# A W added beside the second layer: when its two weights are multiplied, and who makes the denominators

## The chip, the cores and the metric

The kernel runs on one core of a Trainium2 chip. The metric is device time in microseconds (us) of one execution; three executions of the kernel before are at hand. Engines: TensorE (PE; PEld is its weight load), VectorE (DVE), ScalarE (ACT), GpSimd (POOL) and SyncE (SP, which issues DMAs). Each works through its own queue in order; semaphores join them.

## The reference

Two parts, the second fed by the first.

```python
batch, n_heads, seq, head_dim = (4, 4, 1088, 32)   # r = 8
def phi(x):                       # S1, S2: 8 x 32
    a = np.einsum('rd,bhsd->bhsr', S1, x)
    b = np.einsum('rd,bhsd->bhsr', S2, x)
    return np.einsum('bhsi,bhsj->bhsij', a, b).reshape(*x.shape[:-1], r * r)
q_p, k_p = (phi(q), phi(k))
kv = np.einsum('bhsf,bhsd->bhfd', k_p, v)
z = np.sum(k_p, axis=2)
num = np.einsum('bhsf,bhfd->bhsd', q_p, kv)
den = np.einsum('bhsf,bhf->bhs', q_p, z)[..., None] + 1e-06
attn = num / den
x = attn.transpose(0, 2, 1, 3).reshape(4352, 128)
h = x @ w_in                      # 128 x 2048
g = h - np.tanh(h)
out = g @ w_out                   # 2048 x 128
```

All tensors are float32. Since g @ w_out = x @ (w_in @ w_out) + tanh(-h) @ w_out, the kernel computes a small product W = w_in @ w_out once (as the sum of two bf16 halves, `whi` and `wlo`) and adds x W to the second layer of the tanh.

## The kernel before

The 4352 rows go through in 11 groups of 8 to 16 blocks of 32 rows (`GROUPS`, L304), so a group is 256, 448, 384, 448, 384, 512, 448, 384, 448, 384 and 256 columns wide. A batch is 34 blocks, so groups 0, 3, 5 and 8 are the first that need a new batch's keys.

For a batch (`keys`, `sums_of`): K comes by DMA into `kraw`, VectorE turns it in 32x32 blocks into `kT` (L537), PE projects it (L544), VectorE turns the result into `kab` (L555), VectorE and GpSimd make the 64 products per row into `wk` (L570), and PE sums them with V in 36 matmuls (L609). ACT copies the sums (`kvz`, L617), PE turns them (L620), ACT copies them again (`ndw`, L623). Beside this, a small sum of key products (L581, L593) is reduced (L596) into the weights `wq` of the query projection.

For a group (`project_q`, `q_ab`, `q_products`, `numerators`, `x_of`): VectorE turns Q (L631), PE projects it (L653), VectorE turns the projection into `qq` (L682), multiplies and adds to `dn` (L685, L688). One fp32 matmul with a fixed 0/1 matrix `qsum` adds pairs of 32-row blocks of `dn` (L697); VectorE takes the reciprocal (L700), scales (L704); GpSimd, and in groups called `half` VectorE for one of two halves, multiplies out `qp` (L716); VectorE turns it (L723); PE makes the numerators, which are x (L669); x is cast to bf16 into `xT` (L731), by ACT in the first two groups and by VectorE after that.

Then the layers (`layers`): 16 times a first-layer matmul into one of three PSUM banks (L792), a tanh on ACT into one of 40 slots (L795), and 12 slots later a second-layer matmul that accumulates in one PSUM bank, `acc` (L805). x W is two matmuls with `whi` and `wlo` into the same accumulator (L784), at its front, or at its end in the first group. VectorE turns the result out of `acc` into `osb` (L812), and SP stores it (L818). In the last group the layout is different (`last_rows`, L830).

W is made in the opening: the eight chunks of each half of `w_in` are turned by PE (`linear_turn`, L754), the first half into the bank of `acc`, copied by ACT (L759), multiplied with `w_out` by PE (L768), and split by VectorE into `whi` and `wlo` (L772, L773). The weights come as float32; ACT casts w_in in four pieces (L739), GpSimd w_out in two (L743).

The order on each engine is made when the program is built: every operation has an estimated cost and a due time (`prio`), and a list scheduler places it; `P.line([...])` forces an order by hand over named operations (`x0` is the first group's x, `t0_2` the third tanh of the first group, `ds0` its denominator matmul, `wk00` the first key product). `DUE_W` is the due time of the product W in units of 16 per group. Filler matmuls on a zero tile `wz` (L483, L489, L494) stand where PE would else be idle; the scheduler drops those for which there is no room.

Of the kernel before, what the change touches and what calls it, by code (L numbers as in the profile page):

```python
# [8 lines left out]
ALU = mybir.AluOpType  # L9
# [295 lines left out]
DUE_W = 23  # L305


def bass_polysketch_attn__then__act_tanh_shrink_kernel(nc, q, k, v, S1, S2, moe_w_in, moe_w_out, out):
# [40 lines left out]
    dn = [sb(f"dn{i}", [128, 32]) for i in range(2)]  # L349
    an = [sb(f"an{i}", [128, 32, 4]) for i in range(2)]  # L350
# [11 lines left out]
    osl = sb("osl", [128, 3, 128])  # L362
    osb = [sb(f"osb{i}", [128, G]) for i in range(2)]
# [328 lines left out]
    def q_products(g, T):  # L692
        u, n = g % 2, 2 * groups[g][1]
        m, a = n // 2, qq[u]
        half = g < 2 or g in first
        p_rd, p_an = ps[:, 0, 288:288 + n], ps[:, 1, 256:256 + 4 * m].rearrange("p (n x) -> p n x", x=4)
        P.op("tensor", 200, lambda e: e.matmul(  # L697
            ps[:, 0, 256:256 + n], qsum[:, :, :, :].rearrange("p u y j -> p (u y j)"), dn[u][:, 0:n], start=True, stop=True),
            r=[("qsum",), ("dn", u)], w=[bank[0]], prio=T - 0.5, tag=f"ds{g}")
        P.op("vector", 60 + 8.3 * n, lambda e: e.reciprocal(p_rd, ps[:, 0, 256:256 + n]),  # L700
             r=[bank[0]], w=[bank[0]], prio=T, tag=f"rd{g}")
# [25 lines left out]
    def x_of(g, T):  # L727
        _, nb, x0 = groups[g]
        nh = nb // 2
        early = g < 2  # L730
# [6 lines left out]
    def casts():  # L737
        for x in range(4):
            P.op("scalar", act(512), lambda e, x=x: e.copy(  # L739
                w_in[:, 512 * x:512 * x + 512], w_in_f[:, 512 * x:512 * x + 512]),  # L740
                r=[("w_in_f", x // 2)], w=[("w_in", x)], prio=(-50, -50, 2.5, 5.5)[x], tag=f"cin{x}")
# [5 lines left out]
    def linear_turn(half, T):  # L747
        bv, bk = (ps[:, 2, :], bank[2]) if half else (acc, ka)
# [14 lines left out]
    def linear_product(T):  # L763
        wp, kw = ps[:, 3, 0:128], bank[3]

        def product(e):
# [8 lines left out]
            r=[kw, ("whi",)], w=[("wlo",)], prio=T)  # L775

    def layers(g):
# [10 lines left out]
        for jb in range(NJB):  # L788
# [5 lines left out]
                r=[("w_in", jb // 4), ("xT", g)], w=[kb], prio=s, tag=f"h{g}_{jb}")  # L794
# [5 lines left out]
        if g:  # L800
            lin(True)
        for jb in range(NJB):
# [4 lines left out]
                start=(jb == 0 and not g), stop=(jb == NJB - 1 and bool(g))),  # L807
                r=[("w_out", jb // 8), ("t", ts)], w=[ka], prio=s + LAG)
        if not g:
            lin(False)  # L810
        u = g % 2
        P.op("vector", dve(n), lambda e: e.transpose(out=osb[u][:, 0:n], in_=acc[:, 0:n]),  # L812
             r=[ka], w=[("osb", u)], prio=slot0)
        ob = out.rearrange("(b j c) e -> b j c e", b=B, j=32)
        o = 0
        for b, c, nb in parts:
            for cb in range(4):
                P.op("sync", 4096 * nb / 250, lambda e, b=b, c=c, nb=nb, cb=cb, o=o: e.dma_start(  # L818
                    out=ob[b, :, c:c + nb, 32 * cb:32 * cb + 32],
                    in_=osb[u][32 * cb:32 * cb + 32, 32 * o:32 * (o + nb)].rearrange("p (c x) -> p c x", x=32)),  # L820
                    r=[("osb", u)], sem=f"out{u}", prio=slot0)
            o += nb
# [48 lines left out]
    for g in range(NG):  # L871
# [21 lines left out]
        if g == 1:  # L893
            layers(0)
        for x in range(1, B):
# [11 lines left out]
        if g:  # L907
# [49 lines left out]
```

## Time and profile before

| | us |
|---|---|
| three executions | 106.97, 108.19, 109.53; median 108.19 |
| the profiled execution | 107.36 |
| its span, first to last instruction | 105.6 |
| first tanh starts | 14.79 |
| last tanh ends | 101.81 |
| VectorE busy | 65.9 |

The granted clock of TensorE is 1.0 throughout. In a profile line of a timeline stand the start and the duration in us, engine, source line, operation, output <- input, shape, and a count where several were merged; in brackets the engine's idle time before it and what ended that. The busy time of PE is no measure of how full it is, as matmuls overlap in it; starts that follow each other show the rate.

### The profile page before, as it was taken

How to read it: one execution, taken by the hardware profiler on the slowest of the kernel's cores; microseconds unless marked ns; L12 is line 12 of the kernel's file. 1: busy time of each engine (PE TensorE's matmuls, PEld its weight loads, DVE VectorE, ACT ScalarE, POOL GpSimd, SP SyncE). 2: the span in 40 equal slices, each digit the busy share in tenths (PEclk: the TensorE clock that was granted, in tenths of full speed). 3: DMA queues.
4: the chain of work that ended last, by engine and by line, in shares of the span. 5: the costliest groups of instructions: out<-in, count | busy, mean ns of one | idle time of the engine just before them, and what ended most of it. 6: DMA issues, size and time to landing. Idle time of an engine off the chain costs nothing.

```text
span 105.6 us, 3129 instructions
## 1 busy us (share of the span) xinstructions
PE 101.1 (96%) x1285; PEld 54.0 (51%) x1288; DVE 65.9 (62%) x164; ACT 80.3 (76%) x193; POOL 33.3 (32%) x59
## 2 busy tenths in 40 slices
PE   6999999999999999999999999999999999999990
PEld 4535456583456454546546334454754634545580
DVE  3558996499944599783777478769186547143030
ACT  0004559999957977976989998797698998999950
POOL 5569427061811102870400700395030060120000
PEclk9999999999999999999999999999999999999999
DMA  2999999800199322016995022001400502203233
GB/s 68 313 284 281 361 274 252 228 16 0 34 284 241 139 42 45 6 30 107 302 262 100 0 33 48 0 3 25 67 14 4 89 0 43 35 0 58 35 48 76
DMA packets 23678, 11.21 MB, mean 106 GB/s; under 512 B 17648, under 2 KB 22384, under 8 KB 23664
## 3 DMA queue, kind: packets, MB, share of 16 engines
q1 hardware_dynamic: 20144, 7.44, 30.4%
q10 hardware_dynamic: 3520, 3.57, 11.1%
q8 instruction: 10, 0.16, 0.7%
q14 instruction: 4, 0.03, 0.1%
HBM read 8.78 MB, written 2.23 MB: 104 GB/s over the span
## 4 chain that ended last, share of the span: by engine, by line
PE 88%; ACT 9%; DVE 0%; issue 0%
PE ps L792 28%; PE ps L805 24%; ACT tt L795 8%; PE ps L483 6%; PE ps L669 5%; PE ps L609 4%; PE ps L653 4%; PE ps L784 3%; PE ps L544 3%; PE ps L830 2%; PE ps L697 2%; PE ps L494 1%; PE ps L581 1%; PE ps L768 1%; PE ps L754 1%; PE ps L593 1%
## 5 line engine op out<-in xcount | busy, mean ns | idle before, releaser
L795 ACT ACTIVATE tt<-ps 128x448 bf16<-128x448 f32 (+3 forms) x176 | 73.7, 527 | 8.0 <-PE ps L792 7.2
L792 PE MATMUL ps<-xT,w_in 128*128 128x448 bf16 (+3 forms) x174 | 55.9, 333 | 0.4
L805 PE MATMUL ps<-tt,w_out 128*128 128x448 bf16 (+3 forms) x159 | 49.4, 336 | 0.1
L792 PEld LDWEIGHTS ps<-xT,w_in 128*128 128x128 bf16 x176 | 16.8, 97 | 24.1 <-ACT tt L795 15.0
L716 POOL TENSOR_TENSOR qp<-an,qq 128x384 f32<-128x384 f32 (+3 forms) x17 | 14.5, 854 | 39.1 <-DVE an L704 38.3
L805 PEld LDWEIGHTS ps<-tt,w_out 128*128 128x128 bf16 x160 | 16.4, 102 | 8.2 <-issue 0.4
L570 POOL TENSOR_TENSOR wk<-kab 128x256 f32<-128x256 f32 (+1 forms) x18 | 12.6, 698 | 18.1 <-DVE kab L555 17.0
L723 DVE STREAM_TRANSPOSE qpT<-qp 128x448 f32<-128x448 f32 (+3 forms) x22 | 12.3, 577 | 5.2 <-POOL qp L716 5.0
L812 DVE STREAM_TRANSPOSE osb<-ps 128x448 f32<-128x448 f32 (+3 forms) x10 | 6.0, 598 | 7.8 <-PE ps L792 4.2
L700 DVE RECIPROCAL ps<-ps 128x28 f32<-128x28 f32 (+3 forms) x11 | 3.5, 315 | 10.4 <-PE ps L697 10.4
L682 DVE STREAM_TRANSPOSE qq<-ps 128x448 f32<-128x448 f32 (+3 forms) x11 | 6.3, 577 | 3.2 <-PE ps L653 3.1
L483 PE MATMUL ps<-wz 128*128 128x256 bf16 (+1 forms) x28 | 7.3, 398 | 1.1 <-DVE hmask L460 1.1
L617 ACT ACT_TABLE_LOAD x1 | 1.3, 1283 | 8.3 <-DVE gm L588 8.3
L631 DVE STREAM_TRANSPOSE qT<-qraw 128x256 f32<-128x256 f32 (+2 forms) x12 | 6.4, 531 | 1.2 <-DMA qraw<-in_q_dram 1.1
L731 DVE CAST xT<-ps 128x384 bf16<-128x384 f32 (+3 forms) x9 | 5.5, 608 | 1.3 <-PE ps L669 1.1
L669 PE MATMUL ps<-qpT,ndw 64*32 64x224 f32 (+3 forms) x176 | 6.2, 339 | 0.0
L537 DVE STREAM_TRANSPOSE kT<-kraw 128x576 f32<-128x576 f32 (+1 forms) x8 | 5.5, 722 | 1.0 <-DMA kraw<-in_k_dram 1.0
L653 PE MATMUL ps<-qT,wq 64*32 64x224 f32 (+3 forms) x176 | 6.1, 333 | 0.0
L570 DVE TENSOR_TENSOR wk<-kab,ps 128x512 f32<-128x512 f32 (+1 forms) x8 | 5.1, 638 | 0.0
L609 PE MATMUL ps<-wk,vx 128*32 128x64 f32 x288 | 5.1, 221 | 0.0
L609 PEld LDWEIGHTS ps<-wk,vx 128*32 128x32 f32 x288 | 4.2, 110 | 1.3 <-issue 1.3
L555 DVE STREAM_TRANSPOSE kab<-ps 128x576 f32<-128x576 f32 x4 | 3.1, 783 | 2.3 <-PE ps L544 2.3
(74 smaller groups left out, 82.7 us busy)
## 6 DMA issues: line engine op xcount, KB each, us to landing
kraw<-in_k_dram SPq DMA_DIRECT2D x3, 544.0 KB, 4.7
qraw<-in_q_dram SPq DMA_DIRECT2D x3, 544.0 KB, 6.1
vx<-in_v_dram SPq DMA_DIRECT2D x10, 144.0 KB, 4.0
w_in_f<-in_moe_w_in_dram ACTq DMA_DIRECT2D x2, 512.0 KB, 7.3
w_out_f<-in_moe_w_out_dram ACTq DMA_DIRECT2D x2, 512.0 KB, 8.4
out_dram<-osb SPq DMA_DIRECT2D x16, 56.0 KB, 1.9
out_dram<-osb SPq DMA_DIRECT2D x16, 48.0 KB, 1.8
vx<-in_v_dram SPq DMA_DIRECT2D x4, 112.0 KB, 5.1
```

The source lines that it names most:

```text
L483: P.op("tensor", 213 if x < 16 else 221, lambda e, n=1 if x < 16 else 2: e.matmul(ps[:, 3, 0:256 * n], wz[:, 0:128], wz[:, None, :].to_bro ...
L570: P.op(eng, (dve if eng == "vector" else pool)(64 * n), lambda e: e.tensor_tensor(out=wk[:, t0:t1, :, :].rearrange("p t h (i j) -> p (t h) ...
L609: ins = e.matmul(ps[32 * h:32 * h + 32, sbk, 0:64], vx[i][:, h, t, :], wk[:, t, h, :], start=(t == 0), stop=(t == 8), tile_position=(0, 32 ...
L631: P.op("vector", dve(hi - lo), lambda e, i=b % 2, lo=lo, hi=hi: e.transpose(out=qT[i][:, lo:hi], in_=qraw[i][:, lo:hi]), r=[("qraw", b % 2 ...
L653: ins = e.matmul(o, wq[64 * r:64 * r + 64, b, y, :, :].rearrange("p h x -> p (h x)"), src, start=True, stop=True, tile_position=(64 * r, 3 ...
L669: ins = e.matmul(ps[32 * h:32 * h + 32, 2 + u, 0:32 * nh], ndw[i][64 * u:64 * u + 64, 32 * h:32 * h + 32], src[64 * u:64 * u + 64, h // 2, ...
L682: P.op("vector", dve(16 * n), lambda e: e.transpose(out=a[:, 0:n, :].rearrange("p (r m) x -> p r (m x)", r=2), in_=ps[:, pb[0]:pb[1] + 1:p ...
L716: P.op("vector" if dv else "gpsimd", (dve if dv else pool)(32 * m), lambda e, lo=lo, dv=dv: e.tensor_tensor(out=qp[u][:, lo:lo + m, :].rea ...
L723: P.op("vector", dve(32 * m), lambda e, lo=lo: e.transpose(out=qpT[u][:, 32 * lo:32 * (lo + m)], in_=qp[u][:, lo:lo + m, :].rearrange("p n ...
L792: P.op("tensor", pe(n), lambda e, jb=jb, bk=bk: e.matmul(bk[:, 0:n], w_in[:, 128 * jb:128 * jb + 128], xT[:, t0:t0 + n], start=True, stop= ...
L795: P.op("scalar", act(n), lambda e, ts=ts, bk=bk: e.activation(out=tt[:, ts, 0:n], in_=bk[:, 0:n], func=AF.Tanh, scale=-1.0), r=[kb], w=[(" ...
L805: P.op("tensor", pe(n), lambda e, jb=jb, ts=ts: e.matmul(acc[:, 0:n], w_out[:, jb, :], tt[:, ts, 0:n], start=(jb == 0 and not g), stop=(jb ...
```

## The change

Five things are edited.

- W: both turns of `w_in` are now one due time, `DUE_W - 3` with `DUE_W` = 33 in place of 23, and use PSUM banks 2 and 3; the product uses bank 2. They come after the third group's x, and `acc` is no longer borrowed.
- The first group's x W no longer goes into its accumulator. The second-layer sum is turned into a new buffer `osx`; after W is there, x W is computed into bank 2, turned into `osb`, and GpSimd adds `osx`; then the first group is stored. The second group's x W moves to the end of its accumulation.
- Denominators: except in groups 0, 1, 4 and 7, VectorE copies `dn` with neighbouring 32-row blocks exchanged into PSUM (four copies) and adds `dn` into `sd`, of which it takes the reciprocal. Groups 6 and 9 are added to the `half` groups.
- The first x is cast in two halves, by ACT and VectorE; the second by VectorE; the fourth piece of w_in is cast by GpSimd.
- The orders forced by hand change: among others `wk02`, `u0`, `wk00` in place of `wk00`, `u0`, `wk02`.

```diff
-DUE_W = 23
+DUE_W = 33
+TURNED = (0, 1, 4, 7)
...
-        half = g < 2 or g in first
+        half = g < 2 or g in first or g in (6, 9, )
...
+        if g in TURNED:
+            P.op("tensor", 200, lambda e: e.matmul(
+                ps[:, 0, 256:256 + n], qsum[:, :, :, :].rearrange("p u y j -> p (u y j)"), dn[u][:, 0:n], start=True, stop=True),
+                r=[("qsum",), ("dn", u)], w=[bank[0]], prio=T - 0.5, tag=f"ds{g}")
+        else:
+            def swap(e):
+                for s in range(4):
+                    ins = e.tensor_copy(ps[32 * s:32 * s + 32, 0, 256:256 + n], dn[u][32 * (s ^ 1):32 * (s ^ 1) + 32, 0:n])
+                return ins
+
+            P.op("vector", 4 * 140, swap, r=[("dn", u)], w=[bank[0]], prio=T - 0.5, tag=f"ds{g}")
+            P.op("vector", dve(n), lambda e: e.tensor_tensor(
+                out=sd[u][:, 0:n], in0=dn[u][:, 0:n], in1=ps[:, 0, 256:256 + n], op=ALU.add),
+                r=[("dn", u), bank[0]], w=[("sd", u)], prio=T - 0.5, tag=f"dt{g}")
...
-        early = g < 2
+        if g == 0:
+            for half, eng in ((0, "scalar"), (1, "vector")):
+                P.op(eng, (act if eng == "scalar" else dve)(32 * nh), lambda e, half=half, eng=eng: (e.copy if eng == "scalar" else e.tensor_copy)(
+                    xT[:, x0 + 32 * nh * half:x0 + 32 * nh * (half + 1)], ps[:, 2 + half, 0:32 * nh]),
+                    r=[bank[2 + half]], w=[("xT", 0) if half else ("xT", -1)], prio=T, tag=("x0", "x0b")[half])
+            return
+        early = False
...
-            P.op("scalar", act(512), lambda e, x=x: e.copy(
+            P.op("scalar" if x < 3 else "gpsimd", act(512) if x < 3 else 650, lambda e, x=x: (e.copy if x < 3 else e.tensor_copy)(
...
-        bv, bk = (ps[:, 2, :], bank[2]) if half else (acc, ka)
+        bv, bk = ps[:, 2 + half, :], bank[2 + half]
...
-        wp, kw = ps[:, 3, 0:128], bank[3]
+        wp, kw = ps[:, 2, 0:128], bank[2]
...
+    def first_linear(T):
+        n = 32 * groups[0][1]
+        for x, nm in ((whi, "whi"), (wlo, "wlo")):
+            P.op("tensor", pe(n), lambda e, x=x, nm=nm: e.matmul(
+                ps[:, 2, 256:256 + n], x[:, :], xT[:, 0:n], start=(nm == "whi"), stop=(nm == "wlo")),
+                r=[(nm,), ("xT", 0), ("xT", -1)], w=[bank[2]], prio=T, tag="lin0" + nm)
+        P.op("vector", dve(n), lambda e: e.transpose(out=osb[0][:, 0:n], in_=ps[:, 2, 256:256 + n]),
+             r=[bank[2]], w=[("osb", 0)], prio=T, tag="olin0")
+        P.op("gpsimd", pool(n), lambda e: e.tensor_tensor(
+            out=osb[0][:, 0:n], in0=osb[0][:, 0:n], in1=osx[:, 0:n], op=ALU.add),
+            r=[("osb", 0), ("osx",)], w=[("osb", 0)], prio=T, tag="oadd0")
+        store(0)
...
-                start=(jb == 0 and not g), stop=(jb == NJB - 1 and bool(g))),
+                start=(jb == 0 and g < 2), stop=(jb == NJB - 1 and g != 1)),
...
+        ob, ok = (osb[u], ("osb", u)) if g else (osx, ("osx",))
+        P.op("vector", dve(n), lambda e: e.transpose(out=ob[:, 0:n], in_=acc[:, 0:n]),
+             r=[ka], w=[ok], prio=slot0)
...
-            linear_turn(0, 3)
             warm_more(40, 5001)
-            linear_turn(1, DUE_W - 3)
-            linear_product(DUE_W)
...
+        if g == 2:
+            linear_turn(0, DUE_W - 3)
+            linear_turn(1, DUE_W - 3)
+            linear_product(DUE_W)
+            first_linear(DUE_W + 4)
+            layers(1)
...
-    P.line(["kT00", "wkm", "kT01", "kab0", "kps0", "s2m", "gm0", "qT0", "wk00", "u0", "wk02", "qq0", "au0", "dn0", "qT1",
-            "rd0", "an0_1", "an0_0", "qp00", "qpT00", "qpT01", "qq1", "au1", "dn1", "qT2",
-            "rd1", "an1_1", "an1_0", "qp10", "qpT10", "qpT11", "qq2", "au2", "dn2", "rd2", "an2", "kT10", "kT11", "qpT21", "qpT20", "qT3"])
+    P.line(["kT00", "wkm", "kT01", "kab0", "kps0", "s2m", "gm0", "qT0", "wk02", "u0", "wk00", "qq0", "au0", "dn0", "qT1",
+            "rd0", "an0_1", "an0_0", "qp00", "qpT00", "qpT01", "qq1", "x0b", "au1", "dn1", "qT2",
+            "rd1", "an1_1", "an1_0", "qp10", "qpT10", "qpT11", "x1", "qq2", "au2", "dn2", "ds2", "dt2", "rd2", "an2", "kT10", "kT11", "qpT21", "qpT20", "qT3"])
...
-    P.line(["w0", "h0_2", "ds1", "wt0", "w1", "p2"])
+    P.line(["w0", "h0_2", "ds1", "w1", "p2"])
...
-    P.line(["t0_6", "cin3"])
-    P.line(["t0_5", "wc0"])
-    P.line(["wk03", "wk05", "wk07", "qp01", "cout0", "qp11", "cout1"])
+    P.line(["wk03", "wk05", "wk07", "qp01", "cout0", "cin3", "qp11", "cout1"])
```

More of the change, by code (lines that the diff above doesn't have):

```diff
@@ L775, in linear_product, with store @@
             r=[kw, ("whi",)], w=[("wlo",)], prio=T)
+    def first_linear(T):
[10 more added lines that the diff above has]
+        store(0)
+    def store(g):
+        ob = out.rearrange("(b j c) e -> b j c e", b=B, j=32)
+        o, u = 0, g % 2
+        for b, c, nb in groups[g][0]:
+            for cb in range(4):
+                P.op("sync", 4096 * nb / 250, lambda e, b=b, c=c, nb=nb, cb=cb, o=o: e.dma_start(
+                    out=ob[b, :, c:c + nb, 32 * cb:32 * cb + 32],
+                    in_=osb[u][32 * cb:32 * cb + 32, 32 * o:32 * (o + nb)].rearrange("p (c x) -> p c x", x=32)),
+                    r=[("osb", u)], sem=f"out{u}", prio=NJB * g)
+            o += nb
     def layers(g):
@@ L799, in layers @@
             return last_rows(g)
-        if g:
+        if g > 1:
             lin(True)
```

28 lines of the change are left out of this document (9 added, 19 removed).

## The prediction

> **What bounds the kernel now.** I read the page first: shares of busy time and the chain of waits.
>
> ```profile
> span 105.6 us, 3129 instructions
> ...
> PE 101.1 (96%) x1285; PEld 54.0 (51%) x1288; DVE 65.9 (62%) x164; ACT 80.3 (76%) x193; POOL 33.3 (32%) x59
> ...
> PE 88%; ACT 9%; DVE 0%; issue 0%
> PE ps L792 28%; PE ps L805 24%; ACT tt L795 8%; PE ps L483 6%; PE ps L669 5%; PE ps L609 4%; PE ps L653 4%; PE ps L784 3%; PE ps L544 3%; PE ps L830 2%; PE ps L697 2%; PE ps L494 1%; PE ps L581 1%; PE ps L768 1%; PE ps L754 1%; PE ps L593 1%
> ```
>
> The chain is nearly all TensorE, but a chain that goes back along the queue of PE also counts matmuls that had room. So the second view is the timeline of ACT alone from the first tanh on (start, duration, what, idle before).
>
> ```profile
> 14.79 0.94 ACT L795 ACTIVATE tt<-ps 128x256 bf16<-128x256 f32 x3 [0.38 <-PE ps L792]
> ...
> 16.91 1.06 ACT L759 COPY w_inT<-ps 128x1024 bf16<-128x1024 bf16 x1
> 17.80 0.46 ACT L795 ACTIVATE tt<-ps 128x256 bf16<-128x256 f32 x1
> 18.08 0.68 ACT L739 CAST w_in<-w_in_f 128x512 bf16<-128x512 f32 x1
> 18.59 0.46 ACT L795 ACTIVATE tt<-ps 128x256 bf16<-128x256 f32 x1
> 18.86 0.61 ACT L731 CAST xT<-ps 128x448 bf16<-128x448 f32 x1
> 19.27 2.42 ACT L795 ACTIVATE tt<-ps 128x256 bf16<-128x256 f32 x8
> 21.71 1.01 ACT L759 COPY w_inT<-ps 128x1024 bf16<-128x1024 bf16 x1
> 22.62 4.24 ACT L795 ACTIVATE tt<-ps 128x448 bf16<-128x448 f32 x9
> 27.08 2.73 ACT L795 ACTIVATE tt<-ps 128x448 bf16<-128x448 f32 x6 [0.22 <-PE ps L792]
> ...
> 30.73 0.54 ACT L795 ACTIVATE tt<-ps 128x448 bf16<-128x448 f32 x1 [0.93 <-PE ps L792]
> 32.10 0.27 ACT L617 COPY kvz<-ps 128x128 f32<-128x128 f32 x1 [0.82 <-PE ps L609]
> 32.52 0.49 ACT L795 ACTIVATE tt<-ps 128x384 bf16<-128x384 f32 x1 [0.16 <-PE ps L792]
> ...
> 33.06 4.36 ACT L795 ACTIVATE tt<-ps 128x384 bf16<-128x384 f32 x11
> 37.83 0.49 ACT L795 ACTIVATE tt<-ps 128x384 bf16<-128x384 f32 x1 [0.41 <-PE ps L792]
> ```
>
> Three stages show. From 14.8 to 27 us ACT never rests: the opening is bound by ACT, which does two casts and two copies of the transposed weight among its tanh. From 29.8 to 33 it rests 1.9 us in three holes: PE is behind, with the second batch's sums. Then eleven tanh of the third group run without a break, 4.36 / 11, about 0.39 us each. The rest of the kernel repeats this: a stretch of tanh without a break, then a rest at the turn of the group, as the 0.41 at 37.83.
>
> TensorE's queue at the places that matter, and VectorE's and GpSimd's:
>
> ```profile
> 17.24 0.93 PE L494 MATMUL ps<-wz 128*128 128x256 bf16 x7
> ...
> 18.10 0.61 PE L669 MATMUL ps<-qpT,ndw 64*32 64x224 f32 x16
> ...
> 21.07 0.61 PE L754 MATMUL ps<-identb,w_in 128*128 128x128 bf16 x8
> ...
> 22.84 1.06 PE L768 MATMUL ps<-w_out,w_inT 128*128 128x128 bf16 x16
> ...
> 29.61 0.61 PE L653 MATMUL ps<-qT,wq 64*32 64x224 f32 x16
> ...
> 30.82 1.21 PE L609 MATMUL ps<-wk,vx 128*32 128x64 f32 x72
> ...
> 37.45 0.34 PE L792 MATMUL ps<-xT,w_in 128*128 128x384 bf16 x1
> ```
>
> ```profile
> 1.07 0.41 DVE L462 MEMSET hmask<- 32x1 f32 x4
> ...
> 8.33 0.65 DVE L570 TENSOR_TENSOR wk<-kab,ps 128x512 f32<-128x512 f32 x1
> ...
> 8.90 0.18 DVE L596 TENSOR_REDUCE wq<-ps 128x16 f32<-128x32 f32 x1
> ...
> 9.00 0.40 DVE L570 TENSOR_TENSOR wk<-kab,ps 128x256 f32<-128x256 f32 x1
> ...
> 19.15 0.58 DVE L682 STREAM_TRANSPOSE qq<-ps 128x384 f32<-128x384 f32 x1 [1.42 <-PE ps L653]
> ...
> 20.06 0.28 DVE L688 TENSOR_REDUCE dn<-au 128x24 f32<-128x120 f32 x1
> ...
> 21.15 0.32 DVE L700 RECIPROCAL ps<-ps 128x24 f32<-128x24 f32 x1 [0.81 <-PE ps L697]
> ...
> 21.68 1.36 DVE L537 STREAM_TRANSPOSE kT<-kraw 128x576 f32<-128x576 f32 x2
> ...
> 24.68 0.25 DVE L772 CAST whi<-ps 128x128 bf16<-128x128 f32 x1
> ...
> 25.22 0.78 DVE L555 STREAM_TRANSPOSE kab<-ps 128x576 f32<-128x576 f32 x1
> ...
> 26.08 3.44 POOL L570 TENSOR_TENSOR wk<-kab 128x256 f32<-128x256 f32 x5 [2.47 <-DVE kab L555]
> ...
> 28.03 0.41 DVE L812 STREAM_TRANSPOSE osb<-ps 128x256 f32<-128x256 f32 x1
> ```
>
> Seven filler matmuls on a zero tile (L494) stand at 17.24: PE has time to give away where ACT binds. VectorE rests 1.42 us before 19.15 and is then busy without a break through the second batch's keys.
>
> **Opening, up to the first tanh.** The 256-wide key product now goes before the folded weight's reduction and the 512-wide one behind it: the reduction starts 0.65 - 0.40 = 0.25 us earlier, and the first group's projection waits for it. Two filler matmuls ahead of that projection go, so PE is free in time. The first x is split between ACT and VectorE, worth under 0.1 us; VectorE's half stands before the second group's sums of products and delays those by about what the earlier start gave. I take 0.25: first tanh at 14.54.
>
> **ACT's load up to the second group.** By distances between starts: the fourth cast of w_in (now GpSimd's) 18.59 - 18.08 = 0.51; the second x (now VectorE's) 19.27 - 18.86 = 0.41; the two copies of the transposed weight (moved back) 17.80 - 16.91 = 0.89 and 22.62 - 21.71 = 0.91. Together 2.72, so by ACT alone the second group's tanh would start at 22.62 - 0.25 - 2.72 = 19.65. PE has the work ready: the first group's second-layer matmuls now stand between its first-layer ones where fillers stood, since their accumulator no longer holds the transposed weight. The next bound is the second x: its numerators ran at 18.10 behind fillers and come no earlier now, because the thirteenth first-layer matmul stands ahead of them. They end at 18.71; a copy of 0.61 (ACT's row; VectorE's reads the same bank) ends near 19.4; the first layer and the way from matmul to tanh (37.45 to 37.83, 0.38) give a start at 20.2. That is 2.4 us earlier than before. GpSimd's cast stands behind the first half of w_out and well before the 448-wide product it must not delay; the addition of x W is one more 256-wide GpSimd operation (3.44 / 5 = 0.69), and only the first store waits for it.
>
> **What becomes of those 2.4 us.** The 15 tanh of the second group at about 0.45 end near 27.2, and ACT then makes the two copies (1.8 us) and three more tanh, to 30.3. There it must wait. In the emitted order PE now has projection, sums, weight product and the turn of kvz in one row, and only then three first-layer matmuls. The sums need GpSimd's five products, which begin when VectorE has turned the keys. VectorE's queue before that: out go the two halves of W (25.22 - 24.68 = 0.54); in come the second x (its 0.61, of which some 0.35 falls into the rest before 19.15; 0.25 is left), the first group's transpose into the extra buffer (0.41), and the third group's denominators. The last replaces a wait of 0.81 by four copies of 32 rows and one addition. No such copy is in the trace; bounds are the four 32-row memsets (0.41 for four) and four times the small PSUM reduction (4 x 0.18 = 0.72), plus 0.2 for the addition: 0.6 to 0.9, I take 0.75, nearer the reduction, which also touches PSUM. Net -0.54 + 0.25 + 0.41 - 0.06 = about 0: the keys are turned at 25.2 as before, and GpSimd ends at 29.5 as before. So the front of the queue gained 2.4 us and its tail nothing. The sums, 30.82 before, follow the projection directly: between 29.7 and 30.5 (the turn of w_in, 2 x 0.61 at most, now also stands ahead of them). They take 1.2, the product 0.9 to 1.06, the turn 0.3, and the third tanh of the third group starts between 32.6 and 33.3, against 33.06 + 0.39 = 33.45 before. Gain 0.15 to 0.8; I take 0.5. From there ACT binds both kernels up to the group's turn, where the fourth group's numerators now also wait behind VectorE's transpose of x W (0.41): I keep 0.4.
>
> [...]
>
> **Behind that.** The emitted order from the fourth group's projection on is the old one without the removed matmuls, and with two turns changed. The denominators' matmuls hold 2% of the chain, 2.1 us for 11: seven are worth at most 1.3, and nothing where unbroken tanh follow them. I take 0.3. VectorE has room, since it waited for most of them:
>
> ```profile
> DVE ps L700 <- PE ps L697: 10.4, 7, 2.4
> ...
> 63.44 0.60 ACT L795 ACTIVATE tt<-ps 128x512 bf16<-128x512 f32 x1 [0.19 <-PE ps L653]
> ```
>
> Groups 6 and 9 now make half their products on VectorE; their numerators come two first-layer matmuls earlier, so ACT's rest at that turn (0.19 above, and its like) shrinks: 0.3 for both.
>
> **Sum.** The profiled execution took 107.36, that is 105.6 and 1.76 around it; it stands 0.8 below the median of the three runs, 108.19, which spread from 106.97 to 109.53. 107.36 - 0.4 - 0.3 - 0.3 = 106.4, or -1.0 us.
>
> **Rivals.** (a) The 2.4 us arrive whole. That needs the keys of the second batch about 2 us earlier; for it speaks that kraw is loaded long before (the transpose at 21.68 shows no wait). Against it stands VectorE's row, busy from 19.15. With the later 0.6 it gives 107.36 - 3.0 = 104.4. Chance 0.28. (b) VectorE becomes the bound of the third group. Its transpose into the extra buffer waits for the first group's last second-layer matmul ahead of the addition, the reciprocal and the keys; later the halves of W stand behind the fourth group's reciprocal, and PE stands at x W until they come, with three first-layer banks for ACT. From the point where VectorE reaches the keys later than 25.7, every tenth is a tenth of the sums: 0.4 for the wait of that transpose, 0.2 for the copies, 0.6 for x W, and 0.2 in each of the six later groups give +2.4, so 109.8; half of it 108.5. Chance 0.16. (c) The denominators cost PE nothing and the opening gives all back: no change, 107.3. Chance 0.14. My forecast has 0.42, with a range of its own from 105.6 to 107.0.
>
> **Numbers.** 2% (2.15 us, about what runs of this kernel tell from no change) lies at 105.2 and 109.5. Faster: (a) and the low tail of the forecast, 0.33. Slower: the full size of (b), 0.12. Within: 0.55. The range takes in (a) and half of (b): 104.3 to 108.4.
>
> **What would show it.** In the profile after: first tanh near 14.5; second group's near 20.2; the turn of the second batch's keys near 25.2; a hole in ACT between 30 and 33; sums before 30.6; the thirteenth first-layer matmul of the third group near 37.0 (37.45 before). The forecast is wrong if the keys turn before 24 or after 26, or if the distance from there to the end changes by more than 1 us.

## The result, and the profile after

| | before | after |
|---|---|---|
| median of the first comparison, 21 runs each | 108.43 | 107.18 |
| lowest and highest of them | 106.97, 110.92 | 106.39, 111.08 |
| ratio, 95% interval | | 0.9934 [0.9905, 0.9963] |
| all runs of the study: number, median | 131, 108.39 | 37, 107.22 |
| profiled execution, its span | 107.36, 105.6 | 106.00, 104.2 |
| first tanh starts, last tanh ends | 14.79, 101.81 | 14.26, 99.96 |
| VectorE busy | 65.9 | 74.6 |

The change gains 0.7% by the ratio, 1.2 us by the medians over all runs (108.39 - 107.22). Ratios are of the executions within 1.5% of the fastest of their kernel, medians of all executions. The first profile of the changed kernel was of an execution of 108.17 us; the lines here are of a second one, 106.00 us, the fastest of the 37 runs.

From the page of the changed kernel, the span, TensorE's busy time, the chain by engine, and the group of the new VectorE copies (busy us, mean ns of one, idle before):

```profile
span 104.2 us, 3128 instructions
...
PE 98.7 (95%) x1261; PEld 50.3 (48%) x1264; DVE 74.6 (72%) x206; ACT 79.1 (76%) x191; POOL 32.8 (31%) x59
...
PE 80%; ACT 8%; DVE 8%; issue 1%
...
L707 DVE COPY ps<-dn 32x28 f32<-32x28 f32 (+3 forms) x28 | 5.1, 184 | 0.5
```

VectorE, 0% of the chain before, holds 8% now, and its 28 small copies cost 5.1 us. The same view of ACT as in the prediction, changed kernel (L839 is the tanh, L779 the copy of the turned weight):

```profile
14.26 0.94 ACT L839 ACTIVATE tt<-ps 128x256 bf16<-128x256 f32 x3 [0.45 <-PE ps L836]
15.06 0.63 ACT L759 CAST w_in<-w_in_f 128x512 bf16<-128x512 f32 x1
15.57 2.90 ACT L839 ACTIVATE tt<-ps 128x256 bf16<-128x256 f32 x10
19.17 5.45 ACT L839 ACTIVATE tt<-ps 128x256 bf16<-128x256 f32 x13 [0.70 <-PE ps L836]
...
27.43 1.93 ACT L779 COPY w_inT<-ps 128x1024 bf16<-128x1024 bf16 x2 [0.30 <-PE ps L774]
29.25 1.33 ACT L839 ACTIVATE tt<-ps 128x448 bf16<-128x448 f32 x3
31.06 0.27 ACT L620 COPY kvz<-ps 128x128 f32<-128x128 f32 x1 [0.48 <-PE ps L612]
32.15 0.27 ACT L626 COPY ndw<-ps 128x128 f32<-128x128 f32 x1 [0.82 <-PE ps L623]
32.31 1.26 ACT L839 ACTIVATE tt<-ps 128x384 bf16<-128x384 f32 x3
33.81 3.01 ACT L839 ACTIVATE tt<-ps 128x384 bf16<-128x384 f32 x7 [0.24 <-PE ps L836]
37.09 0.49 ACT L839 ACTIVATE tt<-ps 128x384 bf16<-128x384 f32 x1 [0.27 <-PE ps L836]
...
40.01 5.20 ACT L839 ACTIVATE tt<-ps 128x448 bf16<-128x448 f32 x11 [0.56 <-PE ps L836]
...
97.60 2.36 ACT L839 ACTIVATE tt<-ps 128x256 bf16<-128x256 f32 x8
```

ACT, which never rested from 14.8 to 27 before, now rests ahead of 19.17, for a first-layer matmul of TensorE. Three tanh of the first group are left at 19.17; the second group's first, inside that merged row, starts at 20.15, 2.5 us earlier than 22.62. By 30.6 ACT has run dry, and up to 32.2 it rests twice, waiting for the second batch's sums and their turn: the 2.5 us are mostly given back. The fourth group's tanh without a break starts at 40.01, against this row of the kernel before, same view:

```profile
40.94 5.40 ACT L795 ACTIVATE tt<-ps 128x448 bf16<-128x448 f32 x11 [0.56 <-PE ps L792]
```

So 0.93 is won up to there. From that instant to the end of the last tanh it was 101.81 - 40.94 = 60.87 and is 99.96 - 40.01 = 59.95: 0.92 more. The span shrank by 1.4 and not by 1.85; the rest went at the very end, in SyncE's queue of stores (start, duration of the issues). Before, then after:

```profile
95.44 7.26 SPq L818 DMA_DIRECT2D out_dram<-osb  x8
102.74 0.66 SPq L841 DMA_DIRECT2D out_dram<-osl  x1
```

```profile
93.59 8.04 SPq L815 DMA_DIRECT2D out_dram<-osb  x8
101.67 0.66 SPq L879 DMA_DIRECT2D out_dram<-osl  x1
```

SyncE's half of the last store left 102.74 - 101.81 = 0.93 us after the last tanh, and leaves 101.67 - 99.96 = 1.71 after it, as the eight issues ahead of it take 8.04 in place of 7.26. The tail from the last tanh to the end grows from 3.79 to 4.24.

VectorE, changed kernel, between the second and the third group (L634 turns Q, L714 is the reciprocal, L751 the cast of the second x):

```profile
14.40 0.58 DVE L634 STREAM_TRANSPOSE qT<-qraw 128x384 f32<-128x384 f32 x1
14.90 0.31 DVE L714 RECIPROCAL ps<-ps 128x28 f32<-128x28 f32 x1
...
18.70 0.62 DVE L751 CAST xT<-ps 128x448 bf16<-128x448 f32 x1 [1.25 <-PE ps L672]
...
20.45 0.77 DVE L707 COPY ps<-dn 32x24 f32<-32x24 f32 x4
21.13 0.43 DVE L857 STREAM_TRANSPOSE osx<-ps 128x256 f32<-128x256 f32 x1
21.59 0.18 DVE L711 TENSOR_TENSOR sd<-dn,ps 128x24 f32<-128x24 f32 x1
21.80 0.31 DVE L714 RECIPROCAL ps<-sd 128x24 f32<-128x24 f32 x1
...
25.31 0.74 DVE L558 STREAM_TRANSPOSE kab<-ps 128x576 f32<-128x576 f32 x1
```

The keys (`kab`) turn at 25.31; before, at 25.22. What VectorE saved in waits it spends on the second x, the copies and `osx`. And the first profile, same view, one row:

```profile
17.06 0.58 DVE L634 STREAM_TRANSPOSE qT<-qraw 128x384 f32<-128x384 f32 x1 [1.98 <-DMA qraw<-in_q_dram]
```

There the third part of Q landed 10.5 us after its issue (8.0 in the profile above, 8.2 before). This turn stands in VectorE's queue ahead of the second group's reciprocal, so everything behind it came some two us later. The keys and the fourth group there, in a third profile of the changed kernel, and the keys in a second profile of the kernel before:

```profile
27.50 0.74 DVE L558 STREAM_TRANSPOSE kab<-ps 128x576 f32<-128x576 f32 x1
...
42.19 5.21 ACT L839 ACTIVATE tt<-ps 128x448 bf16<-128x448 f32 x11 [0.56 <-PE ps L836]
```

```profile
27.21 0.74 DVE L558 STREAM_TRANSPOSE kab<-ps 128x576 f32<-128x576 f32 x1
...
41.89 5.21 ACT L839 ACTIVATE tt<-ps 128x448 bf16<-128x448 f32 x11 [0.56 <-PE ps L836]
```

```profile
25.25 0.77 DVE L555 STREAM_TRANSPOSE kab<-ps 128x576 f32<-128x576 f32 x1
```

Behind the keys the profiles of one kernel agree. From the turn of the keys to the fourth group's row it was 40.94 - 25.22 = 15.72 and, in the second profile, 40.99 - 25.25 = 15.74; it is 40.01 - 25.31 = 14.70, 42.19 - 27.50 = 14.69 and 41.89 - 27.21 = 14.68. From there to the last tanh's end it was 60.87 and 60.86 and is 59.94 to 59.95 in all three. So 1.03 and 0.92 us are won behind the keys in every profile; what differs between the executions that were profiled lies ahead of the keys and in the tail.

### The profile page after: what moved, and what is told of

The parts are those of the page before. It is cut to its first block, busy times and chain, and to the rows that moved or that the text cites. A ratio compares the mean times of both kernels' runs of the same rounds, so it can differ in the third digit from the quotient of the medians.

```text
span 106.4 us, 3128 instructions
## 1 busy us (share of the span) xinstructions
PE 99.3 (93%) x1261; PEld 50.4 (47%) x1264; DVE 74.7 (70%) x206; ACT 79.2 (74%) x191; POOL 32.8 (31%) x59
## 4 chain that ended last, share of the span: by engine, by line
PE 66%; DMA 13%; DVE 9%; ACT 6%; ACTq 2%; issue 1%
PE ps L836 24%; PE ps L849 22%; DMA qraw<-in_q_dram 10%; ACT tt L839 6%; PE ps L672 4%; PE ps L828 3%; PE ps L656 3%; DMA kraw<-in_k_dram 3%; PE ps L612 2%; PE ps L868 2%; PE ps L547 2%; DVE ps L707 1%; DVE qpT L737 1%; DVE qq L685 1%; ACTq L449 1%
## 5 line engine op out<-in xcount | busy, mean ns | idle before, releaser
L839 ACT ACTIVATE tt<-ps 128x448 bf16<-128x448 f32 (+3 forms) x176 | 72.8, 527 | 7.9 <-PE ps L836 7.6
L836 PE MATMUL ps<-xT,w_in 128*128 128x448 bf16 (+3 forms) x174 | 55.1, 333 | 0.9 <-ACT tt L839 0.7
L836 PEld LDWEIGHTS ps<-xT,w_in 128*128 128x128 bf16 x176 | 16.9, 98 | 26.4 <-ACT tt L839 16.7
L730 POOL TENSOR_TENSOR qp<-an,qq 128x384 f32<-128x384 f32 (+3 forms) x15 | 12.7, 846 | 37.1 <-DVE an L718 36.1
L857 DVE STREAM_TRANSPOSE osb<-ps 128x448 f32<-128x448 f32 (+2 forms) x9 | 5.6, 623 | 10.6 <-PE ps L849 6.4
L634 DVE STREAM_TRANSPOSE qT<-qraw 128x256 f32<-128x256 f32 (+2 forms) x12 | 6.4, 531 | 2.0 <-DMA qraw<-in_q_dram 2.0
L751 DVE CAST xT<-ps 128x448 bf16<-128x448 f32 (+3 forms) x10 | 6.1, 607 | 1.6 <-PE ps L672 1.4
L707 DVE COPY ps<-dn 32x28 f32<-32x28 f32 (+3 forms) x28 | 5.1, 184 | 0.5
## 6 DMA issues: line engine op xcount, KB each, us to landing
w_out_f<-in_moe_w_out_dram ACTq DMA_DIRECT2D x2, 512.0 KB, 10.3
```

Source lines behind the costliest of these rows:

```text
L634: P.op("vector", dve(hi - lo), lambda e, i=b % 2, lo=lo, hi=hi: e.transpose(out=qT[i][:, lo:hi], in_=qraw[i][:, lo:hi]), r=[("qraw", b % 2 ...
L730: P.op("vector" if dv else "gpsimd", (dve if dv else pool)(32 * m), lambda e, lo=lo, dv=dv: e.tensor_tensor(out=qp[u][:, lo:lo + m, :].rea ...
L836: P.op("tensor", pe(n), lambda e, jb=jb, bk=bk: e.matmul(bk[:, 0:n], w_in[:, 128 * jb:128 * jb + 128], xT[:, t0:t0 + n], start=True, stop= ...
L839: P.op("scalar", act(n), lambda e, ts=ts, bk=bk: e.activation(out=tt[:, ts, 0:n], in_=bk[:, 0:n], func=AF.Tanh, scale=-1.0), r=[kb], w=[(" ...
```

## The experiments

The question was which part gains: the opening, the denominators or the new place of W; and whether a late landing of Q's third part takes some of it back. Of each run stand below the ratio to the kernel before (95% interval) and, from its profile, the landing of Q's third part after its issue, the start of the fourth group's unbroken tanh (40.94 before), and the time from there to the last tanh's end, the rest (60.87 before). The rest hardly depends on the loads: it is 60.86 or 60.87 in four profiles of the kernel before and 59.94 or 59.95 in five of the changed one, in each case with two whose load was moved. A tenth means something there. The start of the fourth group moves with the opening, by two us and more.

**The changed kernel again.**

> The changed kernel once more, for a second profile. The ratio should repeat 0.993. The profile taken first had the third part of q land 10.5 us after its issue, at 17.0, and VectorE waited 1.98 us for it. If that landing differs from execution to execution, this profile shows another landing, and with it another start of the second group's numerators (20.17 there); by the prediction's working (no wait for loads) they start at 18.1 and the second group's first tanh at 20.2.

0.9893 [0.9814, 0.9972], median 107.34. This is the profile shown above: landing 8.0, fourth group 40.01, rest 59.95.

**The denominators and the two `half` groups alone**, on the kernel before.

```diff
+TURNED = (0, 1, 4, 7)
-        half = g < 2 or g in first
+        half = g < 2 or g in first or g in (6, 9)
...
+        if g in TURNED:
```

> The kernel before with the denominators of seven groups by VectorE and groups 6 and 9 among the half groups; W and the opening as before. The prediction gave 0.3 us to the denominators and 0.3 to the two groups: 0.6 less, ratio 0.994. Rival: the seven matmuls stood in room that PE had, and the copies cost only VectorE: ratio 0.998 or above.

1.0054 [0.9999, 1.0110]. Landing 8.0, 41.41, 60.14. The ratio is on the rival's side, but not for its reason alone: behind the fourth group the stretch is 0.7 shorter; in front it loses 0.5. No gain in all.

**The new place of W and GpSimd's addition alone.**

```diff
-DUE_W = 23
+DUE_W = 33
...
-        bv, bk = (ps[:, 2, :], bank[2]) if half else (acc, ka)
+        bv, bk = ps[:, 2 + half, :], bank[2 + half]
...
+    def first_linear(T):
```

> The product W made behind the third group's x and the first group's x W added by GpSimd; denominators, half groups, the first two x, the casts and the forced orders of the opening as before. By the prediction ACT gains 1.8 us at the front and loses nearly all of it in the hole behind the second batch's sums: ratio 0.997 to 1.000. Rival: most of the whole change's gain is here (0.994), since TensorE fills its opening with second-layer matmuls. The third possibility is a loss (1.005 or above), because turn and product now stand where PE is short.

1.0137 [1.0068, 1.0205]. Landing 9.4, 43.34, 60.66. Slower; but the scheduler put the second group's x W behind the fourth group's numerators. TensorE stands 1.33 us ahead of these, until VectorE has turned their products, and ACT rests 2.24 us ahead of 39.70, which the whole change does not do. The ratio is thus a bound on nothing but this order. The rest is 0.2 shorter than before, and it is in the eleven tanh of the fourth group, which take 5.20 us in place of 5.40.

**The opening's edits alone**: the casts of x and of w_in, and the forced orders.

```diff
-        early = g < 2
+        early = False
...
-    P.line(["wk03", "wk05", "wk07", "qp01", "cout0", "qp11", "cout1"])
+    P.line(["wk03", "wk05", "wk07", "qp01", "cout0", "cin3", "qp11", "cout1"])
```

> The kernel before with only the opening's edits: key products in the new order, first x in two halves, second x by VectorE, fourth piece of w_in cast by GpSimd. By the prediction 0.25 us from the order and 0.9 us less on ACT, of which little arrives: ratio 0.996 to 0.999. Rival (loads): the third part of q lands no earlier, VectorE's queue waits for it in front of the second group's reciprocal, and the ratio is 1.00.

0.9917 [0.9866, 0.9968], a larger gain than the 0.996 to 0.999 expected. Landing 9.1, 41.22, 60.86: the stretch behind is untouched, and the median of 107.59 is near that of the whole change. In the profile the load comes late, and the fourth group too; counted from the turn of Q's third part, which waits for the load here, it is 41.22 - 15.49 = 25.73, against 40.94 - 14.63 = 26.31 before.

**The turn of Q's third part moved back on VectorE**, behind the second group's products, in the changed kernel and in the opening alone.

```diff
-            "rd0", "an0_1", "an0_0", "qp00", "qpT00", "qpT01", "qq1", "x0b", "au1", "dn1", "qT2",
-            "rd1", "an1_1", "an1_0", "qp10", "qpT10",
+            "rd0", "an0_1", "an0_0", "qp00", "qpT00", "qpT01", "qq1", "x0b", "au1", "dn1",
+            "rd1", "an1_1", "an1_0", "qp10", "qT2", "qpT10",
```

> The changed kernel with one entry moved in VectorE's forced order: the turn of the third group's q goes behind the second group's own product, no longer in front of its reciprocal. Loads theory: in the profiles so far that turn starts when the third part of q lands (14.4 to 17.06, 8.0 to 10.5 us after issue), and everything behind it shifts with it. Then the second group's reciprocal starts near 14.9 whatever the landing, the spread of the times falls, and the ratio to before goes from 0.99 to 0.98. Rival: the slow executions come from elsewhere, and the ratio stays at 0.99.

> The kernel before with the opening's edits (0.9917) and the same move of the turn of the third group's q. If the changed placement of W and the changed denominators are worth nothing, this ties with the changed kernel with the same move, near 0.985. If the front that they free was only spoiled by late loads, it is slower than that one by 0.5% or more.

0.9970 [0.9922, 1.0019] and 0.9930 [0.9874, 0.9987]: no better than without the move. In the first, landing 9.0, the first tanh came only at 15.73, with the same work ahead of it, as TensorE was slow up to 10.3 us (the fillers shown in the last section take 1.25 and 1.01 us there); in the second, landing 7.8, the fourth group started at 40.39. Neither profile has a landing of 10 us or more, so whether the move cures one is not shown. The spread did fall: none of the twelve executions of the first took more than 107.89, while 7 of the 37 of the changed kernel did.

**Fewer denominators by VectorE in the changed kernel**: those of the last groups back to TensorE, then all.

```diff
-TURNED = (0, 1, 4, 7)
+TURNED = (0, 1, 4, 5, 6, 7, 8, 9, 10)
```

```diff
-TURNED = (0, 1, 4, 7)
+TURNED = tuple(range(11))
...
+    P.line(["l1wlo", "w3"])
```

> The changed kernel with the denominators of groups 5, 6, 8, 9 and 10 by TensorE again; groups 2 and 3 stay with VectorE, so the order up to the fourth group is the changed one. By the prediction's 0.3 us for seven, five are worth some 0.2 us: ratio 0.991 to 0.995. Rival: they stand where unbroken tanh hide them, or the shorter way over VectorE costs nothing and gains nothing: the changed kernel's ratio within 0.2%.

> The changed kernel with all denominators by TensorE, and x W of the second group forced in front of the fourth group's numerators as in the changed kernel; groups 6 and 9 stay half groups. By the prediction 0.3 us slower than the changed kernel (ratio to before 0.994 to 0.996). Rival: VectorE's copies in front of the second batch's keys cost more than the wait that they replace, and this is faster than the changed kernel (below 0.988).

0.9924 [0.9878, 0.9969] and 0.9957 [0.9908, 1.0005]. Rest behind the fourth group: 60.30 and 60.36, against 59.95 with all seven on VectorE. So the last five denominators are worth 0.35 us; those of groups 2 and 3 stand ahead of this stretch, which can say little of them. With no denominator on VectorE it is still 0.5 shorter than before. Both kernels keep two more edits that bear on it: the new place of W, worth 0.2 behind the fourth group when it stood alone (60.66), and the two `half` groups, for which 0.3 to 0.4 is left. No run has the `half` groups alone; but with the denominators and without W's move they gave 60.14, which is 0.73, and 0.35 + 0.35 fits that.

**The load of Q's third part issued earlier on ACT's queue**, behind the first half of w_in, in both kernels, and issued last in the changed one.

```diff
+    load_q(0, -2967, groups[0][1] + groups[1][1], CB, "scalar")
...
-    load_q(0, -2955, groups[0][1] + groups[1][1], CB, "scalar")
```

> The changed kernel with one load moved: the third part of q is issued behind the first half of w_in, in front of both halves of w_out; all engines' orders are the same. Loads theory: it lands some 2 us earlier, VectorE no longer waits for it, and the ratio to before goes from about 0.993 to 0.985; the second group's reciprocal starts near 14.9 in the profile. Rival: where the time of the changed kernel scatters, it is not this load, and the ratio stays at 0.993.

> The kernel before with the same load moved. Loads theory, if the kernel before has room behind that load because ACT bounds its opening: no change, 0.998 to 1.000. If both kernels hang on it: 0.990 to 0.995, and the change's gain beside it is not a matter of loads.

> The changed kernel with that load issued last on ACT's queue, behind the second half of w_out. Loads theory: it lands 2 to 3 us later than in the changed kernel, and the time grows by nearly that: ratio to before 1.01 to 1.02. Rival: other work fills the wait, and the ratio stays below 1.00.

0.9886 [0.9826, 0.9947], 0.9967 [0.9916, 1.0018] and 1.0123 [1.0025, 1.0221]. Earlier, the load lands 7.2 and 6.5 us after its issue and VectorE does not wait, yet the medians hardly move (107.20, 108.20). For the kernel before that is no clean test: the second half of w_in is now issued behind that load, and ACT waits 1.28 us for it.

```profile
16.61 0.62 ACT L739 CAST w_in<-w_in_f 128x512 bf16<-128x512 f32 x1 [1.28 <-DMA w_in_f<-in_moe_w_in_dram]
```

Last, it lands 10.5 after a later issue, VectorE waits 2.02, and the fourth group starts at 42.97; by the ratios the kernel loses 2.4% (1.0123 against 0.9886). From ACT's and VectorE's timelines of that kernel:

```profile
7.33 4.14 ACTq L444 DMA_DIRECT2D qraw<-in_q_dram  x1
```

```profile
17.84 0.58 DVE L634 STREAM_TRANSPOSE qT<-qraw 128x384 f32<-128x384 f32 x1 [2.02 <-DMA qraw<-in_q_dram]
...
28.28 0.74 DVE L558 STREAM_TRANSPOSE kab<-ps 128x576 f32<-128x576 f32 x1
```

The move has a second effect: the issue itself holds ACT's queue for 4.14 us (0.57 in the profile of 106.00), and the first tanh comes at 15.72. But it is the landing that sets the keys: they come 28.28 - 17.84 = 10.44 behind the turn of Q's third part, as in the first profile of the changed kernel (27.50 - 17.06 = 10.44), where ACT was not held, and in the third (27.21 - 16.76 = 10.45). A late landing costs; the usual one costs little.

**Everything but the new place of W and VectorE's denominators in groups 2 and 3**: the opening, the two `half` groups, and VectorE for the denominators of groups 5, 6, 8, 9 and 10, on the kernel before.

```diff
+TURNED = (0, 1, 2, 3, 4, 7)
-        half = g < 2 or g in first
+        half = g < 2 or g in first or g in (6, 9)
...
-        early = g < 2
+        early = False
```

> The kernel before with the opening's edits, the half groups 6 and 9, and the denominators of groups 5, 6, 8, 9 and 10 by VectorE: the change without the new place of W and without VectorE's denominators in groups 2 and 3. By the parts measured so far (opening 0.9917; 0.5 us or so from the late groups) 0.986 to 0.990 if the new place of W is worth nothing. If it carries part of the gain, this is at 0.992 or above.

0.9876 [0.9837, 0.9916]. In its profile the load landed only 11.7 us after its issue and VectorE waits 3.29 for it, so the fourth group comes at 44.15; behind the keys, at 28.62, that is 15.53. The rest is 60.14.

**Last, the base and the comparison itself.** Four kernels side by side: the kernel before against itself, the kernel before with the load issued last, the changed kernel, and the one without W's move.

```diff
-    load_q(0, -2955, groups[0][1] + groups[1][1], CB, "scalar")
+    load_q(0, -2945, groups[0][1] + groups[1][1], CB, "scalar")
```

> The kernel before, unchanged, as a run of its own beside further runs of itself. Theory A (the prediction failed in its base: 107.36 less 1.0 was set against one execution that stood under its median): ratio 1.000 with an interval that holds 1, median near 108.4, and a second profile whose span lies elsewhere than 105.6 (between 105 and 108) although no instruction differs; the opening's landing of the third part of q and the length of the key projection differ from 8.2 and 1.57 us, and the stretch from the group turn at 40.94 on to the last tanh stays at 60.87 within 0.3. Theory B (the kernel before is steady, and the changed kernel is what scatters): span within 0.3 of 105.6.

> The kernel before with the load of the third part of q issued last on ACT's queue, as was done to the changed kernel, where it cost 1.0123 against the kernel before (about 2 per cent against the changed kernel). One second-layer matmul of the first group also moves ahead of the second group's numerators. Theory A (both kernels have the turn of that part of q ahead of the second group's reciprocal, and pay for a late landing alike): ratio 1.015 to 1.025, and VectorE waits 1.5 to 2.5 us for the load. Theory B (the kernel before hides a late landing behind ACT, which is busy with casts and copies until 27 us): ratio within 1.005, the second group's tanh and the rest of the group turn no later than in the kernel before by more than 0.5 us.

> The changed kernel a third time, on the chip of the run below, for the comparison with it. Theory A: ratio 0.985 to 0.995. With the load landing 8 to 9 us after its issue the span is 104 to 105.5.

> The kernel before with the opening's edits, VectorE for the denominators of groups 5, 6, 8, 9 and 10, and groups 6 and 9 among those with half their products on VectorE; W is made where the kernel before makes it, and x W of the first group is as before. Theory A (moving W adds nothing to the opening's edits): ratio 0.985 to 0.993, not above that of the changed kernel in the same call by more than 0.003. Theory B (the first reading was luck of the opening's load): above that of the changed kernel by 0.005 or more.

The kernel before against itself gives 0.9930 [0.9885, 0.9975]: the interval leaves out 1 though no instruction differs. A single ratio within some 0.007 of 1 is therefore no finding here, the 0.9934 of the first comparison and five of the ratios above among them. Theory A missed on the span too, which is 105.6 again, as theory B had it, and the fourth group starts where it did. From the timelines of the kernel before, second profile, VectorE and ACT:

```profile
14.66 0.58 DVE L631 STREAM_TRANSPOSE qT<-qraw 128x384 f32<-128x384 f32 x1 [0.36 <-DMA qraw<-in_q_dram]
```

```profile
40.99 5.41 ACT L795 ACTIVATE tt<-ps 128x448 bf16<-128x448 f32 x11 [0.56 <-PE ps L792]
```

The two profiles of this kernel agree, then. But the second is of 107.42 us, with a median of 108.05 in its ten runs: both profiles lie low in the scatter, which reaches from 106.76 to 111.89, and 115 of all 131 runs took longer than the 107.36 from which the prediction counted. So theory A holds in what it says of the base. What makes the slower executions slower stands in neither profile. What holds between the kernels is the set of medians: 107.18, 107.34 and 107.30 of the changed one, each below every one of the kernel before, 108.05 to 108.73.

With the load last, the kernel before took 112.70, 4% over the 108.29 beside it, by medians of 4 and 19 runs; the changed kernel had 110.65. But three of the four had a mean granted clock of 0.981 to 0.985 (two of four, at 0.984, in the changed kernel); the one at 0.997 took 110.16, 1.7% over. VectorE, ACT and TensorE of the profiled execution, the slowest of the four (114.35), and the granted clock from its page (each digit a fortieth of the span, in tenths):

```profile
19.60 0.58 DVE L631 STREAM_TRANSPOSE qT<-qraw 128x384 f32<-128x384 f32 x1 [3.80 <-DMA qraw<-in_q_dram]
```

```profile
23.63 0.53 ACT L731 CAST xT<-ps 128x448 bf16<-128x448 f32 x1 [2.92 <-PE ps L669]
```

```profile
22.71 0.86 PE L669 MATMUL ps<-qpT,ndw 64*32 64x224 f32 x16 [3.02 <-DVE qpT L723]
```

```profile
PEclk9999999958999999999999999999999999999999
```

VectorE waits 3.80 us for the load, TensorE then 3.02 for VectorE, and ACT 2.92 for the second x that follows from it. Behind TensorE's wait the granted clock stands at 0.51 between 23.0 and 26.4 us, and those sixteen matmuls take 0.86 us where they took 0.61. So the 4% hold a loss of clock besides the wait. The wait was longer than the 1.5 to 2.5 us of theory A, and the execution at nearly full clock lies in its range of 1.015 to 1.025. The kernel before does not hide a late landing behind ACT's casts: theory B is refuted, and both kernels pay for a late landing.

The changed kernel gave 0.9884 [0.9837, 0.9931], with a landing of 10.4 in its profile, the fourth group at 41.89 and a rest of 59.95, and the one without W's move 0.9841 [0.9768, 0.9914], of four runs; over all runs their medians are 107.22 (37 runs) and 107.21 (16). In this second profile of the latter, landing 8.2, ACT's timeline shows the fourth group at 40.25:

```profile
32.30 4.36 ACT L814 ACTIVATE tt<-ps 128x384 bf16<-128x384 f32 x11
...
40.25 5.40 ACT L814 ACTIVATE tt<-ps 128x448 bf16<-128x448 f32 x11 [0.56 <-PE ps L811]
```

Of the 0.93 up to the fourth group, 0.69 are there without W's move, and 60.15 behind it against 59.95. But 0.31 of the 0.69 lie ahead of the keys, which turn at 24.91 in this profile; behind them it is 40.25 - 24.91 = 15.34, against 15.72 before and 14.70 in the whole change. Behind the keys, then, W's new place and VectorE's denominators of groups 2 and 3 do give 0.6 to 0.8 us, and 0.2 in the rest, which the medians do not show. By the medians the simpler version is as fast; none of the runs beat it with certainty.

## Why the prediction was right or wrong

The sign and the chain of instants were right; the predicted time was not: 106.4 against 107.2, and 1.2 us of gain between the medians.

- **The step that failed is the base of the sum.** "107.36 - 0.4 - 0.3 - 0.3 = 106.4" subtracts 1.0 from an execution that 115 of 131 runs exceed. Against the median of 108.43 a time of 106.4 asks for a gain of 2.0, twice what the terms hold. From the median that the prediction itself quoted, 108.19, the same terms give 107.2, which was measured. The 0.8 between the two was noted and not used. The second profile of the kernel before stood as low (107.42).
- **That the terms add up to the right size is in part luck.** With the keys in place, all of the 1.0 had to come behind them. From the keys to the end of the span it was 80.4 in both profiles of the kernel before and is 78.9, 78.9 and 79.4 in the three of the changed one: 1.0 to 1.5. The terms were too small, as shown below, and the tail, which takes back 0.5 to 1.0, was in none.
- **Opening.** First tanh forecast at 14.54; 14.26 in the profile shown, but 14.82 and 15.69 in the two others of the same kernel. The 0.25 is smaller than what the opening varies by.
- **ACT's relief, and the second group at 20.2**: 20.15. That x and its cast are the next bound there is what the 1.25 us rest of VectorE ahead of 18.70 shows.
- **"The front of the queue gained 2.4 us, its tail nothing."** Right for the keys: 25.31 (25.2 forecast). Sums at 29.78 and the thirteenth first-layer matmul at 36.72 on TensorE:

```profile
29.78 1.21 PE L612 MATMUL ps<-wk,vx 128*32 128x64 f32 x72
...
36.72 0.34 PE L836 MATMUL ps<-xT,w_in 128*128 128x384 bf16 x1
```

The forecast was 29.7 to 30.5 and 37.0. This speaks against rival (a), whose keys had to come 2 us earlier, and rival (b), whose keys had to come after 25.7 without a late load and which lost time behind them; against (c), in which the denominators cost nothing, stand the 0.35 us below. Behind the keys, up to the fourth group, I kept 0.4; 1.03 came, in every profile. The sums came 1.0 earlier, at the early end of their range, the third tanh of the third group at 32.31, ahead of its range (32.6 to 33.3), and the rests at the group's turn shrank (0.27 at 37.09, where 0.41 stood).
- **Copies.** I took 0.75 for four copies and the addition; 0.77 + 0.18 = 0.95. A copy took 184 ns in the mean, and in the trace of the first profile each of the four began 13 to 14 ns after the end of the one before: the upper bound, four whole durations, was the right one. The keys came at 25.31 all the same.
- **Behind the fourth group.** 0.3 for the `half` groups and 0.3 for the denominators were forecast. Up to the last tanh 0.92 came: some 0.35 from the `half` groups, 0.35 from the denominators, and 0.2 from W's new place, to which the prediction gave nothing there. The tail grew by 0.45 in the profile shown; in the four other profiles with the changed kernel's orders it is 4.3 to 4.8 long, where the kernel before has 3.7 to 3.8 in all four of its own. So 0.5 or less was left of the 0.92.
- **The signs of failure** that were written down came. Keys after 26 were met in the first and the third profile (27.50 and 27.21), by a cause that the prediction missed: Q's third part. The row of before showed it: the load, issued at 6.42, lands 8.2 us later, and the turn starts at 14.63. That no wait stands in brackets there meant that it had landed just in time. And the distance from the keys to the end changed by more than 1 us, 1.5 in two profiles of three, as said above.

One slip of the prediction changes nothing: half of rival (b) is 108.6, not 108.5.

Open are: why the landing varies from 6.5 to 11.7 us; what each of SyncE's last store issues waits for, and so why the tail grows; how W's move and the front's two denominators share the 0.6 to 0.8 us behind the keys (with W moved and every denominator on TensorE it is 41.22 - 26.01 = 15.21), as the scheduler places the neighbours anew in each variant; and what the executions that have no profile, most of those behind the medians, do ahead of the keys.

## What to carry to other kernels

Count a change from the median of the runs and not from one profiled execution, which can lie low in the scatter, as both of the kernel before did here, and compare the kernel with itself once before reading a ratio of 0.993. Where the total scatters, look for a stretch that repeats from profile to profile: here everything from the second batch's keys to the last tanh did, to 0.02 us, and the parts of the change could be weighed there. When an engine ahead is relieved, follow the chain to the next instant that does not move: 2.5 us at the second group became 0.9 two groups later, because the keys stayed where they were. And a DMA that lands just as its reader starts, as the load did here for the turn at 14.63, shows no wait in the profile, yet it bounds every reordering in front of that reader.

## What the runs showed of the hardware

The same 192 KB load landed between 6.5 and 11.7 us after its issue: 7.8 to 11.7 where the order of issues was left as it was, 8.0, 10.4 and 10.5 in three profiles of one kernel. Issued last on ACT's queue, its issue took 4.14 and 3.64 us there, and ACT did nothing else in that time.

With the load last, TensorE stood still for 3.02 us in one execution of the kernel before; right behind that the granted clock was 0.51 of full speed for some 3.4 us, as shown above.

The 16 matmuls of the first key projection, which start at 4.5 to 4.9 us in all profiles, took 1.02 us in one of the changed kernel and 1.51 in another; 1.57 and 1.39 in the two of the kernel before. From the timelines of TensorE, the changed kernel in its second and its third profile:

```profile
4.79 1.02 PE L547 MATMUL ps<-kT,wkm 64*32 64x288 f32 x16
```

```profile
4.75 1.51 PE L547 MATMUL ps<-kT,wkm 64*32 64x288 f32 x16
```

Fillers on the zero tile, three of 256 columns and two of 512, in the same two profiles:

```profile
6.16 0.71 PE L486 MATMUL ps<-wz 128*128 128x256 bf16 x3
...
7.71 0.60 PE L486 MATMUL ps<-wz 128*128 128x512 bf16 x2
```

```profile
6.91 1.25 PE L486 MATMUL ps<-wz 128*128 128x256 bf16 x3
...
9.35 1.04 PE L486 MATMUL ps<-wz 128*128 128x512 bf16 x2
```

The same matmuls take 1.7 times as long in the third profile, until about 10.3 us, and its first tanh comes at 15.69 in place of 14.26. The row of the granted clock shows 9 in the slices of the opening on both pages, so it does not tell this: the trace's records of the clock begin only at 5.10 us in the second profile and at 10.29 in the third, and the page shows the time without a record as full. In the first profile of the kernel before they begin at 6.55, so its clock of 1.0 is known from there on.

No run tested the cause of the slow opening.
